# Gelu in phases on ScalarE, and Strassen's scheme for all but the first two token groups

## The chip, the cores and the metric

The kernel runs on one core of one Trainium2 chip. The metric is the time of the device in microseconds (us), median of the runs. A core has five engines that run beside each other and wait for one another through semaphores: TensorE (PE, matmuls; its weight loads are listed as PEld), VectorE (DVE), ScalarE (ACT), GpSimd (POOL) and SyncE (SP, which here issues stores). Each engine works through its own instructions in program order.

## The reference

Attention with causal mask over 8 batches, 8 heads, 576 tokens of 64 values, with 16 extra keys and values ("beacons") in front that every token sees; then a layer of two matrices with a gelu between, for all 4608 tokens.

```python
# q, k, v: (8, 8, 576, 64); beacon_k, beacon_v: (8, 8, 16, 64)
k_all = np.concatenate([beacon_k, k], axis=2)
v_all = np.concatenate([beacon_v, v], axis=2)
scores = scale * np.matmul(q, k_all.transpose(0, 1, 3, 2))      # scale = 1/8
scores = np.where(causal, -1e9, scores)
a = np.exp(scores - scores.max(-1, keepdims=True))
a /= a.sum(-1, keepdims=True) + 1e-09
attn = np.matmul(a, v_all)
x = attn.transpose(0, 2, 1, 3).reshape(4608, 512)

h = x @ w_in                                                    # (4608, 2048)
g = h * (1.0 / (1.0 + np.exp(-1.702 * h)))
out = g @ w_out                                                 # (4608, 512), float32
```

## The kernel before

The kernel is one Python function that first lists operations with their dependences, a guessed duration and a priority, lets a small planner (`Plan.run`) put them in order, and then writes the instructions in that order. The order on each engine is therefore fixed when the kernel is built; on the chip only semaphores move things.

The attention goes by 16 sets (a batch and four of its heads). The scores of a set are cut into chunks of at most 512 columns for each of the four heads; there are 55 chunks. A chunk is a burst of small matmuls (`qk`, L388) into one score tile, and one or two exponentials (L399) from it:

```python
pss = ctx.enter_context(tc.tile_pool(name="pss", bufs=1, space=bass.MemoryType.PSUM))
psu = ctx.enter_context(tc.tile_pool(name="psu", bufs=1, space=bass.MemoryType.PSUM))
RING = 4                                   # psu tiles u0..u3, [128, 512] f32 each
...
sc = pss.tile([P, Q, 512], F32, tag="s", name="s")
...
nc.scalar.activation(out=Es[s][:, :, c0:c1], in_=ss[i][...], func=AFT.Exp, scale=0.125)
```

There is one score tile, so the matmuls of a chunk wait for the exponential of the chunk before. All other matmul results go to a ring of four tiles `u`. GpSimd (and VectorE early on) masks the exponentials (L420), VectorE adds them up for the denominators (`zadd`, L451), and the value matmuls (`av`, L473) follow with transposes for the reciprocals (L484 to L493) and a multiplication (`norm`, L502) into `xT`, the input of the first layer.

The two layers go by ten groups of tokens: two of 256 (0 and 1), then eight of 512 (2 to 9). First layer (`m1`, L526): 16 tiles of 128 x 512 for a group of 512 tokens, four matmuls each. Then either tanh on ScalarE and a gate on VectorE, or gelu on ScalarE alone:

```python
def e_tanh(g, n0, n1):                                          # L540
    nc.scalar.activation(out=sig[:, 0:w], in_=rings[("m1", g, n0)][:, 0:w], func=AFT.Tanh, scale=0.851)
def e_gate(g, n0, n1):                                          # L559: (tanh + 1) * u
    nc.vector.scalar_tensor_tensor(out=gts[g][...], in0=sig, scalar=1.0, in1=u, op0=ALU.add, op1=ALU.mult)
def e_gelu(g, n0, n1):                                          # L547
    nc.scalar.activation(out=gts[g][...], in_=u, func=AFT.Gelu_apprx_sigmoid)
```

Groups from `GEL` on take gelu. Tanh and Exp share a table of ScalarE; gelu is in another, and the kernel before switches once, after the last exponential.

Second layer: a plain group takes 64 matmuls of 512 columns (`m2`, L571) and an evacuation on ScalarE (L584) for each 128 tokens. Groups from `NPL` up to `NPE` take Strassen's scheme: the 512 x 2048 by 2048 x 512 product is cut in quarters and made of seven products of 256-column matmuls (L640) in place of eight, with sums of quarters of `g` (`e_s`, L591, 16 pieces a group on VectorE) and of `w_out` (`e_t`, once), and joins of the results on VectorE (L656, seven a group) beside one halving on ScalarE (L651):

```python
NPL, NPE, GEL = 6, 10, 7
...
lhs, rhs = {
    1: (quarter(g, 0, 0), w(0, 0)), 2: (quarter(g, 0, 1), w(1, 0)), 3: (sA[2], w(1, 1)),
    4: (quarter(g, 1, 1), tb(2)),   5: (sA[0], tb(0)),   6: (sA[1], tb(1)),   7: (quarter(g, 1, 0), tb(3)),
}[p]
for n in range(n0, n1):
    for mt in range(2):
        nc.tensor.matmul(u[:, HM * mt : HM * (mt + 1)], lhs[:, n, mt * P : (mt + 1) * P], rhs[:, n, :], ...)
```

The chunks are spread by due times, so that the attention lasts until about two thirds of the span, with the layers of earlier tokens between them:

```python
T_ATT0, T_ATT1 = 13000, 235000            # ns; due time of chunk i rises evenly between them
```

Of the kernel before, what the change touches and what calls it, by code (L numbers as in the profile page):

```python
# [10 lines left out]
ALU = mybir.AluOpType  # L11


NEAR = 140


class Op:
    __slots__ = (
        "eng", "dur", "deps", "pr", "due", "emit", "kind", "ring", "mode", "lat",
        "start", "end", "left", "users", "ready", "seq", "name", "tail",  # L20
    )


class Plan:
# [5 lines left out]
    def __init__(self, ring):  # L30
        self.ops = []
        self.bank = [None] * ring
        self.tiles = {}
        self.closers = {}

    def op(self, eng, dur, deps, emit, kind="", pr=5, due=0, ring=None, closes=None, mode=None, name="", tail=0):
        o = Op()
        o.eng, o.dur, o.emit, o.kind, o.pr, o.due = eng, dur, emit, kind, pr, due
        o.ring, o.mode, o.name, o.tail = ring, mode, name, tail
# [23 lines left out]
    def run(self):  # L63
        free = {e: 0 for e in ("PE", "ACT", "DVE", "POOL", "Q", "SP")}
        free.update(POOL=900, SP=700)
        avail = {e: [] for e in free}
        for o in self.ops:
            if o.left == 0:
                avail[o.eng].append(o)
        mode, last, tail = "m", "", 0  # L70
        order = []
        todo = len(self.ops)
        while todo:
            best = None
            slot = self.ring_free()
            ringt = slot[0] if slot else None
            for e, cand in avail.items():
                t = None
                for o in cand:
                    r = max(o.ready, o.due)  # L80
# [12 lines left out]
            ok = []  # L93
            for o in avail[e]:
                r = max(o.ready, o.due)
                if o.ring is not None and o.ring not in self.tiles:
                    if ringt is None:
                        continue
                    r = max(r, ringt)
                if r <= t:  # L100
                    ok.append(o)
            if e == "PE":
                o = self.choose(ok, t, mode, last, free)
            else:
                o = min(ok, key=lambda o: (o.pr, o.ready, o.seq))
                if e == "DVE" and o.pr > 0:
                    near = [x for x in avail[e] if x.pr == 0 and max(x.ready, x.due) <= t + NEAR]
                    if near:
                        o = min(near, key=lambda o: (o.ready, o.seq))
                        t = max(t, o.ready, o.due)  # L110
            dur = o.dur
            if e == "PE":
                if o.mode != mode:
                    dur += 95 + 0.75 * tail / 2.4
                mode, last, tail = o.mode, o.kind, o.tail
                if o.ring is not None and o.ring not in self.tiles:
                    self.tiles[o.ring] = slot[1]
                    self.bank[slot[1]] = o.ring
            o.start, o.end = t, t + dur
# [17 lines left out]
    def choose(self, ok, t, mode, last, free):  # L137
        def first(kinds, test=lambda o: True):
            c = [o for o in ok if o.kind in kinds and test(o)]
            return min(c, key=lambda o: (o.pr, o.seq)) if c else None  # L140
# [9 lines left out]
                return av  # L150
        if qk:
            return qk
        late = first(("av",), lambda o: o.ready + 8000 <= t)
        if late:
            return late
        m1, m2 = first(("m1",)), first(("m2",))
        if m1 and m2:
            return m2 if last == "m1" or free["ACT"] > t + 1500 else m1
        return m1 or m2 or av
# [3 lines left out]
def kernel(  # L163
# [47 lines left out]
    w1t = cst.tile([P, NKT, DFF], F16, tag="w1", name="w1")  # L211
    w2t = cst.tile([P, NNT, DMODEL], F16, tag="w2", name="w2")
    XR = 4 * S
    NPL, NPE, GEL = 6, 10, 7
    HM, HN = 256, NNT // 2
    xT = cst.tile([P, NKT, XR], F16, tag="xT", name="xT")
    sA = [cst.tile([P, HN, HM], F16, tag=f"sA{i}", name=f"sA{i}") for i in range(3)]
# [375 lines left out]
    def tb(i):  # L593
        if i < 3:
            return tB[i][:, :, :]
        return bkf[:, :, :].bitcast(F16).rearrange("p s e -> p (s e)").rearrange("p (n w) -> p n w", w=HM)

    def e_t(i, eng):
        b11, b12 = w2t[:, 0:HN, 0:HM], w2t[:, 0:HN, HM:]
# [65 lines left out]
            in_=osbs[(g, i)][:, :].rearrange("p (a n) -> p a n", a=2),  # L665
        )

    T_ATT0, T_ATT1 = 13000, 235000
    NCH0 = 4 * HS
    T_CH = (T_ATT1 - T_ATT0) / (len(CHUNKS) - NCH0)  # L670

# [54 lines left out]
    def turns(s):  # L726
        urgent = s < HS
        cast = op(
            "DVE", 80, ld_bk[s] + [turn.get((s - 2, 1))], lambda: e_bk(s),
            pr=0 if urgent else 4, due=max(8800 * s if s < HS else 26000, due_of(s) - 10000), name=f"bk{s}",  # L730
        )
        bkc[s] = cast
        for which in (1, 0):
# [7 lines left out]
    def chunk(i):  # L741
# [6 lines left out]
        if i:  # L748
# [2 lines left out]
        w = sum(max(45, 2 * x / 2.4 + 6) for x in ps)  # L751
        qks[i] = op(
            "PE", w, deps, lambda: e_qk(i), kind="qk", pr=0,
            due=T_ATT0 + T_CH * (i - NCH0) if i >= NCH0 else 0, mode="r", name=f"qk{i}", tail=ps[-1],
        )
        for n, (s, c0, c1) in enumerate(CHUNKS[i]):
            x = exps[(i, n)] = op(
                "ACT", 140 + 0.833 * 4 * (c1 - c0), [qks[i]], lambda n=n: e_exp(i, n), pr=0, name=f"exp{s}.{i}"
            )
            parts.setdefault(s, []).append((c0, c1, x))  # L760
            for m, (j, a, e) in enumerate(MASKS):
# [9 lines left out]

    def after(s, c0, c1):
        return [x for u, v, x in parts[s] + masks.get(s, []) if u < c1 and v > c0]

    def values(s):
        b, hs = divmod(s, HS)
# [23 lines left out]
        for n, (x, half) in enumerate(order):  # L800
# [15 lines left out]
            )  # L816
            if x == 2:
                z1 = op("DVE", 410, [avs[(s, x, half)]], lambda h=half: e_z1(s, h), pr=0, closes=key, name="z1")
                z2[half] = op("DVE", 600, [z1], lambda h=half: e_z2(s, h), pr=0, name="z2")
            else:  # L820
                norms[(s, x, half)] = op(
                    "DVE", 380, [avs[(s, x, half)], z2[half]], lambda x=x, half=half: e_norm(s, x, half),
                    pr=1 if s >= HS else 0, closes=key, name="norm",
                )
# [34 lines left out]
    for j in range(-1, NJ):  # L859
        load_v(1, j)  # L860

    m1s, done, tanhs, gelus = {}, {}, [], []
    SQ, SDVE, TDUE = 2, 0, 200000

    def weights():
        prev = []
        for i in range(4):
            prev = [op("DVE", 1450, w2_ld + prev, lambda i=i: e_t(i, "DVE"), pr=3, due=TDUE, name="t")]
            tds[i] = prev[0]

    tds = {}

    def products(g):
        eng = "POOL" if g < SDVE else "DVE"
# [41 lines left out]
            op("SP", 60, [o], lambda: e_store4(g, i, r, c), name="store")  # L916

        prod(1)
        half = op("ACT", 560, [last[1]], lambda: e_half(g, 1, "m"), pr=1, closes=("p", g, 1), name="half")
        prod(2)  # L920
        c11 = join(2, "m", "a", [half])
        store(c11, "a", 0, 0)
# [11 lines left out]
        prod(3)  # L934
        c12 = join(3, "m", "m", [u4])
        store(c12, "m", 0, 1)

    def mlp(g):
        if g == NPL and NPL < NPE:
# [4 lines left out]
        for hb in range(t0 // HF, (t1 - 1) // HF + 1):  # L944
            b, half = divmod(hb, 2)
            for hs in range(HS):
                for x in range(2):
                    xs.append(norms[(HS * b + hs, x, half)])
        old = done.get(g - 2, [])
        n = 512 // w  # L950
        late = list(tanhs[-16:]) if g >= GEL else []
        firsts = list(range(0, NNT, n))
        if NPL <= g < NPE:
            firsts.sort(key=lambda n: (n % HN // SQ, n))
        for n0 in firsts:
# [6 lines left out]
            m1s.setdefault(g, []).append(pe)  # L962
            if g >= GEL:
                gates[(g, n0)] = op(
                    "ACT", 555 if gelus else 1840, [pe] + late, lambda n0=n0, n1=n1: e_gelu(g, n0, n1),
                    pr=1, closes=key, name="gelu",
                )
                gelus.append(gates[(g, n0)])
                continue
            a = op("ACT", 555, [pe], lambda n0=n0, n1=n1: e_tanh(g, n0, n1), pr=1, name="tanh")  # L970
            tanhs.append(a)
# [41 lines left out]
        o.left += 1  # L1013
        d.users.append(o)

    for o in bkc.values() if tds else ():
        also(tds[3], o)
    for o in gelus[:1]:
        for d in exps.values():
            also(o, d)  # L1020
    for o in gelus[1:]:
        also(o, gelus[0])
    order = plan.run()
    for o in order:
        o.emit()
# [29 lines left out]
```

## Time and profile before

| | before |
|---|---|
| time, median of 3 runs | 341.72 us (341.63 to 343.0) |
| span of the profiled run | 339.7 us, TensorE clock 0.999 |
| plain second layer (L571) | 320 matmuls of 512 columns |
| Strassen's products (L640) | 448 matmuls of 256 columns |
| gates on VectorE (L559) | 96, mean 678 ns |
| sums of quarters of `g` (L591) | 64, median 419 to 422 ns |
| joins (L656) | 28, mean 690 ns |
| tanh (L540), gelu (L547) | 96 of 598 ns, 48 of 597 ns |
| evacuations (L584) | 20, mean 598 ns |
| exponentials (L399) | 66, 98.8 us in all |

The page gives for each engine the time in which it was busy and its share of the span; then the span in 40 equal slices, one digit each, the busy share in tenths; then the chain of work that ended last, followed back from the last instruction, with the shares of engines. A row of the order in time gives start, length, engine, line, operation, output and inputs with their shapes, a count, and in brackets the idle time before it and what ended it. A row of the windows gives the stretch, its length, then busy time and count for PE, PEld, DVE, ACT and POOL, the granted clock, the share of DMA and GB/s. The modelled length of a matmul is longer than its distance to the next; distances between starts are the better measure.

### The profile page before, as it was taken

The page shows a single profiled execution, that of the slowest core. Times are in us where ns is not written, and L with a number is a line of the kernel's source. Part 1 is how long each engine was busy: PE and PEld are TensorE (multiplying, and loading weights), DVE is VectorE, ACT ScalarE, POOL GpSimd, SP SyncE. Part 2 cuts the span into 40 slices and gives each one's busy share as a digit, 9 for nine tenths or more (in the row PEclk, how much of TensorE's full clock was granted, in tenths as well). Part 3 has the DMA queues.
Part 4 walks back from the last instruction along what each step waited for, and adds up shares of the span by engine and source line. Part 5 has one row for each costly group of instructions (what it writes and reads, how often), then busy time and mean ns, then how long its engine had stood idle before and what let it go on. Part 6 is the DMA issues. An engine that isn't in the chain of part 4 may idle for free.

```text
span 339.7 us, 10091 instructions
## 1 busy us (share of the span) xinstructions
PE 318.0 (94%) x4360; PEld 196.9 (58%) x4360; DVE 246.8 (73%) x502; ACT 196.7 (58%) x236; POOL 117.5 (35%) x190
## 2 busy tenths in 40 slices
PE   0699898999889999999999999999999999999995
PEld 0475676544455455455566765455556766766784
DVE  3847869699989698897988999987762361371293
ACT  1585686778755776677767767767553244244200
POOL 8765585393245217442912563131100000000000
PEclk9999999999999999999999999999999999999999
DMA  7999999493419155905965191000000010010022
GB/s 129 159 206 208 194 204 139 97 92 83 67 41 138 36 102 59 147 33 102 84 94 101 40 150 51 31 35 33 33 0 33 32 64 31 33 63 33 32 95 93
DMA packets 56173, 28.84 MB, mean 85 GB/s; under 512 B 41280, under 2 KB 49472, under 8 KB 56128
## 3 DMA queue, kind: packets, MB, share of 16 engines
q0 software_dynamic: 47552, 18.49, 46.4%
q1 hardware_dynamic: 8512, 9.69, 8.2%
q8 instruction: 34, 0.56, 0.7%
q14 instruction: 11, 0.09, 0.1%
q10 hardware_dynamic: 64, 0.01, 0.0%
HBM read 37.22 MB, written 9.44 MB: 137 GB/s over the span
## 4 chain that ended last, share of the span: by engine, by line
PE 79%; DMA 9%; DVE 7%; POOL 2%; issue 1%; ACT 0%; DVEq 0%; POOLq 0%
PE u L526 32%; PE u L571 19%; PE u L640 14%; PE u L473 8%; PE s L388 7%; DMA w<-in_moe_w_in_dram 5%; DMA w<-in_moe_w_out_dram 4%; DVE g L559 2%; DVE zs L451 2%; DVE osb L656 1%; DVE xT L502 1%; DVE rz L493 1%; POOL vb L319 1%; POOL E L420 0%; ACT E L399 0%
## 5 line engine op out<-in xcount | busy, mean ns | idle before, releaser
L526 PE MATMUL u<-xT,w 128*128 128x512 f16 (+1 forms) x704 | 147.7, 341 | 1.2 <-DVE zt L484 0.5
L399 ACT ACTIVATE E<-s 128x2048 f16<-128x2048 f32 (+4 forms) x66 | 98.8, 1514 | 29.3 <-PE s L388 28.4
L526 PEld LDWEIGHTS <-w 128*128 128x128 f16 x704 | 66.3, 98 | 48.6 <-issue 1.3
L420 POOL TENSOR_SCALAR_AFFINE_SELECT E<-E 128x512 f16<-128x512 f16 (+3 forms) x90 | 53.1, 623 | 108.2 <-ACT E L399 97.9
L540 ACT ACTIVATE sig<-u 128x512 f16<-128x512 f32 x96 | 57.2, 598 | 45.2 <-PE u L526 42.4
L571 PE MATMUL u<-w,g 128*128 128x512 f16 x320 | 81.5, 380 | 0.4 <-DMA w<-in_moe_w_out_dram 0.3
L559 DVE SCALAR_TENSOR_TENSOR g<-sig,u 128x512 f16<-128x512 f16 x96 | 64.3, 678 | 20.6 <-ACT sig L540 20.2
L656 DVE SCALAR_TENSOR_TENSOR osb<-u,osb 128x512 f32<-128x512 f32 x28 | 18.9, 690 | 48.1 <-PE u L640 37.1
L547 ACT ACTIVATE g<-u 128x512 f16<-128x512 f32 x48 | 28.7, 597 | 43.1 <-PE u L526 43.0
L571 PEld LDWEIGHTS <-g 128*128 128x128 f16 x320 | 29.7, 98 | 31.9 <-issue 0.9
L388 PE MATMUL s<-qT,kT 32*128 32x32 f16 (+9 forms) x1544 | 35.9, 225 | 13.0 <-DVE qT L359 11.2
L388 PEld LDWEIGHTS <-kT 32*128 32x128 f16 x1544 | 28.5, 94 | 33.0 <-issue 20.7
L473 PE MATMUL u<-E,vb 128*32 128x288 f16 (+4 forms) x1024 | 29.4, 258 | 1.7 <-DVE g L559 1.2
L640 PEld LDWEIGHTS <-g 128*128 128x128 f16 x256 | 25.0, 98 | 10.4
L451 DVE TENSOR_TENSOR zs<-zs,E 128x192 f16<-128x192 f16 (+3 forms) x48 | 27.2, 568 | 4.2 <-POOL E L420 1.9
L319 POOL DMA_DIRECT2D vb<-in_v_dram x32 | 27.2, 865 | 2.4 <-DMA qn<-in_q_dram 1.2
L502 DVE TENSOR_TENSOR xT<-u,rz 128x288 f16<-128x288 f32 x64 | 26.4, 448 | 2.0 <-PE u L473 1.5
L473 PEld LDWEIGHTS <-vb 128*32 128x32 f16 (+1 forms) x1024 | 22.1, 98 | 5.9 <-issue 3.0
L640 PEld LDWEIGHTS <-sA 128*128 128x128 f16 x192 | 18.8, 98 | 4.7
L359 DVE STREAM_TRANSPOSE kT<-kn 128x576 f32<-128x576 f32 x16 | 20.1, 1258 | 1.9 <-DMA kn<-in_k_dram 1.4
L359 DVE STREAM_TRANSPOSE qT<-qn 128x576 f32<-128x576 f32 x16 | 20.0, 1248 | 0.4 <-DMA qn<-in_q_dram 0.3
L451 DVE TENSOR_TENSOR zs<-E 128x704 f16<-128x704 f16 (+1 forms) x24 | 16.0, 667 | 3.2 <-ACT E L399 2.6
(45 smaller groups left out, 210.0 us busy)
## 6 DMA issues: line engine op xcount, KB each, us to landing
out_dram<-osb SPq DMA_DIRECT2D x36, 256.0 KB, 2.2
kn<-in_k_dram POOLq DMA_DIRECT2D x16, 288.0 KB, 6.6
qn<-in_q_dram POOLq DMA_DIRECT2D x16, 288.0 KB, 6.3
vb<-in_v_dram POOLq DMA_DIRECT2D x24, 128.0 KB, 4.9
w<-in_moe_w_in_dram POOLq DMA_DIRECT2D x8, 256.0 KB, 9.7
w<-in_moe_w_out_dram POOLq DMA_DIRECT2D x4, 512.0 KB, 13.9
vb<-in_v_dram POOLq DMA_DIRECT2D x8, 112.0 KB, 3.7
vb<-in_v_dram POOLq DMA_DIRECT2D x8, 80.0 KB, 4.7
```

The costliest lines, as they stand in the source:

```text
L319: nc.gpsimd.dma_start(out=t[0 : hi - lo, j, h0:h1, :], in_=v[b, h0:h1, lo:hi, :].rearrange("h n d -> n h d"),)
L359: nc.vector.transpose(out=f32(dst.rearrange("p n e -> p (n e)")).rearrange("p (r t) -> p t r", t=TR), in_=f32(src[:, :]).rearrange("p (t c ...
L388: nc.tensor.matmul(sc[:, h, o : o + w], kT[s % NB2][r : r + 32, j * P : (j + 1) * P, d], qT[s % NB2][r : r + 32, a : a + w, d], start=(d = ...
L399: nc.scalar.activation(out=Es[s][:, :, c0:c1], in_=ss[i][:, :, o : o + c1 - c0], func=AFT.Exp, scale=0.125,)
L420: nc.gpsimd.affine_select(out=blk, in_=blk, compare_op=ALU.is_ge, fill=0.0, base=off + (Nb if j == 0 else 0), pattern=[[0, Q], [1, w]], ch ...
L451: nc.vector.tensor_tensor(out=t[:, :, o : o + w], in0=x, in1=y, op=ALU.add)
L473: nc.tensor.matmul(u[32 * h : 32 * h + 32, a:e], lhs, src[0:kw, h, col : col + e - a], start=first, stop=last,)
L526: nc.tensor.matmul(u[:, o + a - t0 : o + e - t0], w1t[:, kp, nt * P : (nt + 1) * P], xT[:, kp, a % XR : (e - 1) % XR + 1], start=(kp == 0) ...
L540: nc.scalar.activation(out=sig[:, 0:w], in_=rings[("m1", g, n0)][:, 0:w], func=AFT.Tanh, scale=0.851)
L559: nc.vector.scalar_tensor_tensor(out=gts[g][:, n0:n1, 0:w], in0=sigs[(g, n0)][:, 0 : n * w].rearrange("p (n w) -> p n w", n=n), scalar=1.0 ...
L571: nc.tensor.matmul(o[:, :], gts[g][:, nt, mt * P : (mt + 1) * P], w2t[:, nt, :], start=(nt == 0), stop=(nt == NNT - 1),)
L640: nc.tensor.matmul(u[:, HM * mt : HM * (mt + 1)], lhs[:, n, mt * P : (mt + 1) * P], rhs[:, n, :], start=(n == 0 and mt == 0), stop=(n == H ...
```

## The change

Strassen's scheme is used for groups 2 to 9 in place of 6 to 9, and gelu on ScalarE for the same groups in place of 7 to 9. It is meant to take matmuls from TensorE and gates from VectorE. As exponentials are still to come while those groups run, ScalarE must switch tables back and forth; so the planner gets phases. In an exponential phase there are chunks, values and second-layer products, but no first layer of the next group; when a given number of chunks is done (`QUOTAS`) and the group's input is ready, a gelu phase follows, with the 16 first-layer tiles of the group and no chunk.

```diff
-NEAR = 140
+NEAR = 260
...
+        def allowed(o):
+            if o.kind == "m2" and o.ring not in self.tiles:
+                if sum(left_of[k] > 0 for k in self.tiles if k in left_of) >= 2:
+                    return False
+            if o.kind == "m1":
+                return o.pr < group or (o.pr == group and (inside or group not in self.quota))
+            if o.kind == "qk":
+                return not inside
+            if o.table is not None and o.table != table:
+                return due_of_table[table] == 0
+            return True
...
+            if not inside and group in self.quota:
+                f = firsts[group]
+                inside = nchunk >= self.quota[group] and f.left == 0
...
+            if o.kind == "m1":
+                ntile += 1 if o.pr == group else 0
+                if inside and ntile == 16:
+                    group, inside, ntile = group + 1, False, 0
...
+                if o.table != table:
+                    dur += 1283
+                    table = o.table
...
-        late = first(("av",), lambda o: o.ready + 8000 <= t)
+        late = first(("av",), lambda o: o.ready + 6000 <= t)
...
+        if m1 and inside:
+            return m1
...
-    NPL, NPE, GEL = 6, 10, 7
+    NPL, NPE, GEL = 2, 10, 2
+    QUOTAS = (20, 26, 32, 41, 48, 55, 55, 55)
...
-        return bkf[:, :, :].bitcast(F16).rearrange("p s e -> p (s e)").rearrange("p (n w) -> p n w", w=HM)
+        return w2t[:, 0:HN, HM:]
...
-    T_ATT0, T_ATT1 = 13000, 235000
+    T_ATT0, T_ATT1 = 13000, 245000
...
-            due=T_ATT0 + T_CH * (i - NCH0) if i >= NCH0 else 0, mode="r", name=f"qk{i}", tail=ps[-1],
+            due=0, mode="r", name=f"qk{i}", tail=ps[-1],
...
-    SQ, SDVE, TDUE = 2, 0, 200000
+    SQ, SDVE, TDUE = 2, 0, 65000
...
-                    "ACT", 555 if gelus else 1840, [pe] + late, lambda n0=n0, n1=n1: e_gelu(g, n0, n1),
-                    pr=1, closes=key, name="gelu",
+                    "ACT", 555, [pe], lambda n0=n0, n1=n1: e_gelu(g, n0, n1),
+                    pr=1, closes=key, name="gelu", table="g",
...
-    for o in gelus[:1]:
-        for d in exps.values():
-            also(o, d)
+    plan.quota.update(zip(range(GEL, NG), QUOTAS))
```

A chunk has no due time of its own any more; the loads and transposes of its set still have. The sums of quarters of `w_out` move from 200 to 65 us in the plan, and the fourth of them now overwrites a quarter of `w_out` that only plain groups need. The rest of the diff passes the new fields along and adds two dependences that the planner had not listed.

More of the change, by code (lines that the diff above doesn't have):

```diff
@@ L19 @@
         "eng", "dur", "deps", "pr", "due", "emit", "kind", "ring", "mode", "lat",
-        "start", "end", "left", "users", "ready", "seq", "name", "tail",
+        "start", "end", "left", "users", "ready", "seq", "name", "tail", "table",
     )
@@ L34, in __init__, with op @@
         self.closers = {}
-    def op(self, eng, dur, deps, emit, kind="", pr=5, due=0, ring=None, closes=None, mode=None, name="", tail=0):
+        self.quota = {}
+    def op(self, eng, dur, deps, emit, kind="", pr=5, due=0, ring=None, closes=None, mode=None, name="", tail=0, table=None):
         o = Op()
         o.eng, o.dur, o.emit, o.kind, o.pr, o.due = eng, dur, emit, kind, pr, due
-        o.ring, o.mode, o.name, o.tail = ring, mode, name, tail
+        o.ring, o.mode, o.name, o.tail, o.table = ring, mode, name, tail, table
         o.deps = [d for d in deps if d is not None]
@@ L70, in run @@
         mode, last, tail = "m", "", 0
+        table, due_of_table = "e", {"e": 0, "g": 0}
+        group, inside, ntile, nchunk = min(self.quota), False, 0, 0
+        firsts = {}
+        for o in self.ops:
+            if o.kind == "m1":
+                firsts.setdefault(o.pr, o)
+        left_of = {}
+        for o in self.ops:
+            if o.kind == "m2":
+                left_of[o.ring] = left_of.get(o.ring, 0) + 1
+        def allowed(o):
[9 more added lines that the diff above has]
+            return True
         order = []
@@ L79, in run @@
                 for o in cand:
+                    if not allowed(o):
+                        continue
                     r = max(o.ready, o.due)
@@ L94, in run @@
             for o in avail[e]:
+                if not allowed(o):
+                    continue
                 r = max(o.ready, o.due)
@@ L102, in run @@
             if e == "PE":
-                o = self.choose(ok, t, mode, last, free)
+                o = self.choose(ok, t, mode, last, free, inside)
             else:
@@ L118, in run @@
                     self.bank[slot[1]] = o.ring
+            if o.kind == "m1":
+                ntile += 1 if o.pr == group else 0
+                if inside and ntile == 16:
+                    group, inside, ntile = group + 1, False, 0
+            if o.kind == "m2":
+                left_of[o.ring] -= 1
+            nchunk += o.kind == "qk"
+            if o.kind in ("m1", "qk"):
+                for u in o.users:
+                    if u.table is not None:
+                        due_of_table[u.table] += 1
+            if o.table is not None:
+                due_of_table[o.table] -= 1
+                if o.table != table:
+                    dur += 1283
+                    table = o.table
             o.start, o.end = t, t + dur
@@ L135, in run, with choose @@
         return order
-    def choose(self, ok, t, mode, last, free):
+    def choose(self, ok, t, mode, last, free, inside):
         def first(kinds, test=lambda o: True):
@@ L729, in turns @@
             "DVE", 80, ld_bk[s] + [turn.get((s - 2, 1))], lambda: e_bk(s),
-            pr=0 if urgent else 4, due=max(8800 * s if s < HS else 26000, due_of(s) - 10000), name=f"bk{s}",
+            pr=0 if urgent else 4, due=max(8800 * s if s < HS else 26000, due_of(s) - 8000), name=f"bk{s}",
         )
@@ L757, in chunk @@
             x = exps[(i, n)] = op(
-                "ACT", 140 + 0.833 * 4 * (c1 - c0), [qks[i]], lambda n=n: e_exp(i, n), pr=0, name=f"exp{s}.{i}"
+                "ACT", 140 + 0.833 * 4 * (c1 - c0), [qks[i]], lambda n=n: e_exp(i, n), pr=0, name=f"exp{s}.{i}",
+                table="e",
             )
@@ L773, in after, with two_back @@
         return [x for u, v, x in parts[s] + masks.get(s, []) if u < c1 and v > c0]
+    zseq = [(s, h) for h in range(2) for s in range(HS)]
+    zseq += [(s, h ^ (s >= ZSUM)) for s in range(HS, NSET) for h in range(2)]
+    def two_back(s, half):
+        i = zseq.index((s, half))
+        return zseq[i - 2] if i > 1 else (-1, 0)
     def values(s):
@@ L818, in values @@
                 z1 = op("DVE", 410, [avs[(s, x, half)]], lambda h=half: e_z1(s, h), pr=0, closes=key, name="z1")
-                z2[half] = op("DVE", 600, [z1], lambda h=half: e_z2(s, h), pr=0, name="z2")
+                z2[half] = op("DVE", 600, [z1] + [norms.get((*two_back(s, half), y)) for y in range(2)], lambda h=half: e_z2(s, h), pr=0, name="z2")
             else:
-                norms[(s, x, half)] = op(
+                norms[(s, half, x)] = op(
                     "DVE", 380, [avs[(s, x, half)], z2[half]], lambda x=x, half=half: e_norm(s, x, half),
@@ L860 @@
         load_v(1, j)
-    m1s, done, tanhs, gelus = {}, {}, [], []
-    SQ, SDVE, TDUE = 2, 0, 200000
+    m1s, done = {}, {}
+    SQ, SDVE, TDUE = 2, 0, 65000
     def weights():
@@ L867, in weights @@
         for i in range(4):
-            prev = [op("DVE", 1450, w2_ld + prev, lambda i=i: e_t(i, "DVE"), pr=3, due=TDUE, name="t")]
+            prev = [op("DVE", 1450, w2_ld + (prev if i < 3 else [tds[0]]), lambda i=i: e_t(i, "DVE"), pr=3, due=TDUE, name="t")]
             tds[i] = prev[0]
-    tds = {}
+    tds, ends = {}, {}
     def products(g):
@@ L918, in products @@
         prod(1)
-        half = op("ACT", 560, [last[1]], lambda: e_half(g, 1, "m"), pr=1, closes=("p", g, 1), name="half")
+        half = op("ACT", 560, [last[1], ends.get(g - 1)], lambda: e_half(g, 1, "m"), pr=1, closes=("p", g, 1), name="half")
         prod(2)
@@ L936, in products @@
         store(c12, "m", 0, 1)
+        ends[g] = c12
     def mlp(g):
@@ L947, in mlp @@
                 for x in range(2):
-                    xs.append(norms[(HS * b + hs, x, half)])
+                    xs.append(norms[(HS * b + hs, half, x)])
         old = done.get(g - 2, [])
         n = 512 // w
-        late = list(tanhs[-16:]) if g >= GEL else []
         firsts = list(range(0, NNT, n))
@@ L964, in mlp @@
                 gates[(g, n0)] = op(
-                    "ACT", 555 if gelus else 1840, [pe] + late, lambda n0=n0, n1=n1: e_gelu(g, n0, n1),
-                    pr=1, closes=key, name="gelu",
+                    "ACT", 555, [pe], lambda n0=n0, n1=n1: e_gelu(g, n0, n1),
+                    pr=1, closes=key, name="gelu", table="g",
                 )
-                gelus.append(gates[(g, n0)])
                 continue
-            a = op("ACT", 555, [pe], lambda n0=n0, n1=n1: e_tanh(g, n0, n1), pr=1, name="tanh")
-            tanhs.append(a)
+            a = op("ACT", 555, [pe], lambda n0=n0, n1=n1: e_tanh(g, n0, n1), pr=1, name="tanh", table="e")
             gates[(g, n0)] = op(
@@ L1014, in also @@
         d.users.append(o)
-    for o in bkc.values() if tds else ():
+    for o in done.get(NPL - 1, []) + done.get(NPL - 2, []) if tds else ():
         also(tds[3], o)
-    for o in gelus[:1]:
-        for d in exps.values():
-            also(o, d)
-    for o in gelus[1:]:
-        also(o, gelus[0])
+    plan.quota.update(zip(range(GEL, NG), QUOTAS))
     order = plan.run()
```

## The prediction

> **What bounds the kernel now.** I read the page from the top: engines and slices first, then the chain that ended last, then windows of the span, and last the order in time of TensorE and ScalarE where the two stages meet.
>
> ```profile
> PE 318.0 (94%) x4360; PEld 196.9 (58%) x4360; DVE 246.8 (73%) x502; ACT 196.7 (58%) x236; POOL 117.5 (35%) x190
> PE   0699898999889999999999999999999999999995
> DVE  3847869699989698897988999987762361371293
> ACT  1585686778755776677767767767553244244200
> ```
>
> TensorE is busy in nearly every slice. Its gaps are at the start (inputs and weights land until about 40 us) and in the last slice. VectorE runs at nine tenths from 60 to 240 us, so it is close behind.
>
> ```profile
> PE 79%; DMA 9%; DVE 7%; POOL 2%; issue 1%; ACT 0%; DVEq 0%; POOLq 0%
> ```
>
> The chain of waits runs through TensorE for 79% and through ScalarE for nothing. The windows say where TensorE has air:
>
> ```profile
> 40.00:130.00 90.00, 85.49 (x1404) 47.92 (x1406) 76.66 (x150) 64.83 (x72) 43.28 (x70) 1.00 0.79 102
> 130.00:240.00 110.00, 109.86 (x1682) 63.99 (x1683) 98.23 (x193) 76.69 (x88) 46.22 (x71) 1.00 0.50 72
> 240.00:317.00 77.00, 77.00 (x569) 49.13 (x568) 32.39 (x78) 32.34 (x54) 0.00 (x0) 1.00 0.10 35
> ```
>
> After the span's limits the first busy figure is TensorE, then weight loads, VectorE, ScalarE, GpSimd. TensorE idles 4.5 us between 40 and 130, 0.14 us between 130 and 240, nothing after. So the last 200 us shrink only if TensorE is given less to do. ScalarE, at 70% in the middle window, and VectorE, at 89%, can give way or get in the way, but saving on them alone moves nothing there.
>
> Lengths of the pieces, and the one place where the kernel already changes ScalarE's table between exponentials and gelu:
>
> ```profile
> 58.80 1.73 PE u L571 x8
> 317.92 15.30 PE u L640 x140
> 57.19 0.64 PE L388 MATMUL s<-qT,kT 32*128 32x288 f16 x24
> 57.96 1.88 ACT L399 ACTIVATE E<-s 128x2048 f16<-128x2048 f32 x1 [0.88 <-PE s L388]
> 244.00 1.28 ACT L547 ACT_TABLE_LOAD   x1
> 245.30 1.29 ACT L547 ACTIVATE g<-u 128x512 f16<-128x512 f32 x2
> ```
>
> Eight matmuls of 512 columns in 1.73 us are 216 ns each; 140 of Strassen's 256 columns in 15.30 us are 109.3 ns each. A chunk of scores takes 0.64 us of TensorE, its exponential begins 0.77 us after the chunk and lasts 1.88 us. The table load takes 1.28 us and the gelu follows at once.
>
> **What the Trainium skill says.** "ScalarE: Activation LUTs", What ACT_TABLE_LOAD costs: about 1283 ns for a load plus about 1380 ns of drain for every switch. The trace agrees with the first (1.28 us) and shows nothing of the second: the evacuation before it ends at 243.99, the load starts at 244.00, the gelu at 245.30. I charge 1.30 us. The same page, Table sets: the hidden batching unit, puts exp and tanh in one set and gelu in another; the trace agrees, as exponentials and tanh alternate without loads. "TensorE: Matmul & The Clock Gate", Back-to-back issue gap, gives N/2.4 + 2.5 ns, so 216 and 109 ns; the trace has 216 and 109.3. Halving the columns costs about 1 ns per matmul here, so nearly the whole of Strassen's saving arrives. "PSUM — Partial Sum Buffer", Specifications: eight banks of 512 FP32 values per partition. The score tile takes four (one buffer) and the ring of four tiles takes the rest, so no second score tile and no longer ring is to be had. That matters below.
>
> **The change part by part.**
>
> Second layer. A plain group is 64 matmuls of 512 columns: 64 x 216 = 13.84 us. With Strassen it is 7 products x 16 matmuls of 256 columns: 112 x 109.3 = 12.24 us. Saved on TensorE: 1.60 us a group. Four more groups (2 to 5): 6.4 us, all on the bound engine. First layer, scores and values keep their matmuls; the changes between the three tilings of the array, counted in the order of both kernels, are 145 before and 147 after, so nothing there.
>
> VectorE. Five groups (2 to 6) lose the gate: 80 x 0.67 us (64.3/96) = 53.6 us off. Four groups gain 16 additions of 0.42 us and 7 joins of 0.69 us: 4 x 11.5 = 46 us on. Net -7 us, about 239 us busy. No relief of note, and the additions stand beside the attention work where before they stood in the quiet last 90 us.
>
> ScalarE. Tanh for gelu is even (598 against 597 ns). Sixteen evacuations fall away and four halvings come: -7 us. The order shows six gelu phases, the last with three groups in it: 12 table loads instead of 2, +12.8 us. ScalarE rises to about 202 us of the span, far from a bound; what counts is where TensorE waits for a load.
>
> Rhythm of an exponential phase (seven chunks in each of the five full ones). One score tile, so the next chunk starts after the exponential: 0.77 + 1.88 + 0.05 = 2.70 us a chunk. The order puts about 20 Strassen matmuls (2.19 us) between two chunks, or values and some of them. TensorE: 0.58 for the chunk to its successor + 2.19 + about 0.1 for the change of tiling = 2.87. TensorE sets the pace by 0.2 us; the few thinner gaps (1.57, 1.82, 1.91) wait a few tenths. I put +0.5 us for all.
>
> Going into a gelu phase. From the start of the last chunk, 0.77 + 1.88 + 1.30 + 0.60 = 4.55 us until the first ring tile comes free. TensorE fills four tiles in 0.65 + 4 x 0.865 = 4.1 us, then waits about 0.5. In the order, two of the six entries have values or a rest of products to bridge this. 4 x 0.5 = +2 us.
>
> Coming out. The last gelu ends about 0.8 us after its matmuls, load 1.3, exponential 1.9: the second chunk can start 4.05 us after the last first-layer matmul. TensorE has one chunk (0.65) and 3.5 to 3.9 us of values and products there, 4.2 or more. Nothing lost.
>
> The stretch up to chunk 20. Groups 0 and 1 keep tanh and gate, group 2 is held back until 20 chunks are done, and the four sums of weights (about 1.5 us each on VectorE) move from 200 to 65 us. Twelve chunks of some 3 us VectorE work each stand here with about 11 gates, so VectorE is the tight engine: +1.5 us. Against it, the waits of TensorE for gates between 79 and 95 us in the kernel before (0.27, 0.58, 0.96, 0.19, about 2 us) go with the gates: -1.5.
>
> VectorE in the periods. One period (chunks and a gelu phase) is on TensorE 13.8 + 12.2 + 7 x 0.7 + values 4 = 35 us; VectorE has some 32 us in it, most of that in the exponential phase, since a join (0.69) must free a ring tile and a sum of exponentials must be ready for the values. I charge a few tenths per period, +1.5 us.
>
> Sum: -6.4 + 0.5 + 2 + 1.5 - 1.5 + 1.5 = -2.4, so 339.3. I think my charges lean to the high side, since the planner that fixes the order knows the load time, the ring and these durations and put bridging work where it could, and before it reached 109.86 of 110 us with VectorE at 89%. I halve the charges for the entries and VectorE's order (3.5 to 1.75) and take 337.4.
>
> **The rivals.**
>
> 1. Full gain: everything is bridged, and the waits before 130 us go too. Then -6.4 and up to -2 more: 333 to 335. For it: TensorE's order has work in each gap. Against: four entries with nothing between the first-layer matmuls and a ring of four.
>
> 2. VectorE becomes the bound in the middle. Its orders are fixed, and 32 us of work in 35 with joins, sums, transposes and additions in one queue lets one late item (a mask from GpSimd, an exponential) hold all behind it. In the trace the in-place sum of 1152 columns takes 996 ns against 779 for the one that writes elsewhere, so its length isn't steady. If it costs 1.5 us a period, 5 x 1.5 = 7.5 us: 342 to 345. For it: 17 to 19.7 us busy of each 20 already. Against: the mean load doesn't rise (53.6 off, 46 on).
>
> 3. ScalarE becomes the bound of the exponential phases. For it: the pace is only 0.2 us below TensorE's. If an exponential starts 0.4 us later than I think in each of 35 chunks, +7 us or more: 342 to 344. Against: 0.77 and 0.05 us are read in stretches where nothing else stood on ScalarE, and in these phases nothing but one halving does.
>
> 4. The loads of q, k and v come in bursts. For it: seven chunks in 20 us instead of one each 4.7. Against: DMA is at a twentieth to a tenth of its time after 80 us, and GpSimd idles half of it. No effect.
>
> **Range and chances.** 337.4, of which the certain part is the 6.4 us. The line for over 2% is 334.9, which leaves all losses together no more than the waits regained: rival 1, a bit over a quarter. Slower by over 2% (348.6) needs rivals 2 and 3 together at full size: one in twenty. Range 333 to 343.
>
> **What the profile would show.** Right: TensorE busy down by about 6 us; 320 plain matmuls of the second layer become 64, Strassen's 448 become 896; waits of the first-layer matmuls for gelu of about 0.5 us, once in each of some four phases; 12 table loads of 1.28 us. Rival 2: TensorE waiting for joins, sums or norms in the exponential phases, with VectorE full. Rival 3: chunks at more than 2.9 us from start to start with ScalarE full. The last 81 us, which I add up to from the order after the last chunk (48 first-layer tiles and 21 products), should be gapless. I am wrong if TensorE idles over 8 us in all after 40 us, or under 2.

## The result and the profile after

The changed kernel takes 333.49 us (333.26 to 333.51, four runs) against 342.36 us for the kernel before on the same chip (341.63 to 343.56, four runs): 0.9736 of the time, 95% interval 0.9702 to 0.977. (The median of three from which the prediction counts is 341.72; the fourth run took 343.56.) The spans of the two profiled runs are 339.7 and 331.8 us, 7.9 us apart.

The lines of the changed kernel's file are others than before: scores L439, exponentials L450, values L524, first layer L577, gelu L598, plain second layer L622, sums of quarters L642, Strassen's products L691 (L693 in e5 and e6), joins L707.

The page of the changed kernel, engines and slices, then the shares of the chain that ended last:

```profile
PE 312.2 (94%) x4552; PEld 215.6 (65%) x4552; DVE 239.8 (72%) x514; ACT 203.1 (61%) x234; POOL 117.3 (35%) x190
PE   0699998999999999999999999999999999999995
DVE  3747867898799779977899688977988600460483
ACT  1586586776866776778668576957676465065000
...
PE 70%; DMA 7%; issue 7%; POOL 7%; ACT 4%; DVE 3%; POOLq 0%; DVEq 0%
```

TensorE's busy time is down by 5.8 us, VectorE's by 7.0, ScalarE's is up by 6.4. Now the windows of the changed kernel (stretch, its length, busy time and count of PE, PEld, DVE, ACT, POOL, clock, DMA):

```profile
0.00:40.00 40.00, 27.69 (x547) 20.29 (x548) 26.55 (x58) 22.12 (x23) 28.11 (x49) 1.00 1.22 181
40.00:80.00 40.00, 37.85 (x602) 22.16 (x601) 31.83 (x58) 29.75 (x35) 23.03 (x36) 1.00 1.14 132
80.00:130.00 50.00, 49.62 (x813) 34.08 (x812) 42.85 (x93) 35.82 (x39) 18.64 (x31) 1.00 0.48 71
130.00:180.00 50.00, 49.72 (x825) 35.89 (x824) 43.77 (x97) 36.92 (x39) 25.16 (x40) 1.00 0.72 95
180.00:230.00 50.00, 50.00 (x742) 36.22 (x740) 40.17 (x90) 35.59 (x43) 14.15 (x23) 1.00 0.48 73
230.00:260.00 30.00, 29.43 (x498) 19.59 (x497) 26.08 (x59) 20.33 (x22) 8.18 (x13) 1.00 0.11 37
260.00:320.00 60.00, 60.00 (x466) 40.51 (x465) 22.28 (x52) 22.58 (x38) 0.00 (x0) 1.00 0.11 36
```

TensorE idles 0.38 us between 80 and 130, 0.28 us between 130 and 180, 0.57 us between 230 and 260 and nothing else up to 320. The kernel before idles 2.61 us between 80 and 130 (47.39 us busy of 50) and 1.90 between 40 and 80 (38.10 of 40). In the first 40 us the two kernels do the same work in nearly the same order; there the changed one idles 0.9 us less (27.69 us busy against 26.83), a difference of the size seen between other kernels of this document in that stretch.

How a gelu phase is entered, in TensorE's order in time and then in ScalarE's (start, length, engine, line, operation, output and inputs, count, and in brackets the idle time before and what ended it):

```profile
103.62 0.64 PE L439 MATMUL s<-qT,kT 32*128 32x176 f16 x32
104.20 3.63 PE L577 MATMUL u<-xT,w 128*128 128x512 f16 x16
108.17 4.04 PE L577 MATMUL u<-xT,w 128*128 128x512 f16 x18 [0.34 <-ACT g L598]
```
```profile
104.33 1.88 ACT L450 ACTIVATE E<-s 128x2048 f16<-128x2048 f32 x1 [1.69 <-PE s L439]
106.23 1.28 ACT L598 ACT_TABLE_LOAD   x1
107.52 3.17 ACT L598 ACTIVATE g<-u 128x512 f16<-128x512 f32 x6
```

The chunk starts at 103.62, its exponential at 104.33, the load at 106.23, the first gelu at 107.52. TensorE fills the four ring tiles with 16 matmuls and goes on at 108.17, which is 4.55 us after the chunk's start. The row shows 0.34 us of idle time, counted from the modelled end of the last matmul; by starts, 16 x 216 ns are over at 107.66, and 0.5 us are lost. Two more of the six entries wait, 0.41 us (at 71.78) and 0.36 us (at 249.50); the other three show no such wait.

### The profile page after: what moved, and what is told of

It reads as the page before. It is cut to its first block, busy times and chain, and to the rows that moved or that the text cites. A ratio compares the mean times of both kernels' runs of the same rounds, so it can differ in the third digit from the quotient of the medians.

```text
span 331.8 us, 10414 instructions
## 1 busy us (share of the span) xinstructions
PE 312.2 (94%) x4552; PEld 215.6 (65%) x4552; DVE 239.8 (72%) x514; ACT 203.1 (61%) x234; POOL 117.3 (35%) x190
## 4 chain that ended last, share of the span: by engine, by line
PE 70%; DMA 7%; issue 7%; POOL 7%; ACT 4%; DVE 3%; POOLq 0%; DVEq 0%
PE u L577 29%; PE u L691 25%; PE u L524 7%; PE s L439 6%; DMA w<-in_moe_w_out_dram 5%; ACT E L450 3%; PE u L622 3%; DMA w<-in_moe_w_in_dram 3%; POOL E L471 2%; POOL vb L370 2%; DVE osb L707 1%; DVE zs L502 1%; POOL qn L354 1%; POOL kn L354 1%; ACT L598 1%
## 5 line engine op out<-in xcount | busy, mean ns | idle before, releaser
L577 PE MATMUL u<-xT,w 128*128 128x512 f16 (+1 forms) x704 | 131.1, 343 | 1.4 <-ACT g L598 1.1
L450 ACT ACTIVATE E<-s 128x2048 f16<-128x2048 f32 (+4 forms) x66 | 98.8, 1514 | 50.7 <-PE s L439 50.0
L577 PEld LDWEIGHTS <-w 128*128 128x128 f16 x704 | 67.6, 98 | 56.9 <-issue 2.4
L598 ACT ACTIVATE g<-u 128x512 f16<-128x512 f32 x128 | 74.4, 599 | 46.0 <-PE u L577 31.7
L707 DVE SCALAR_TENSOR_TENSOR osb<-u,osb 128x512 f32<-128x512 f32 x56 | 37.7, 681 | 39.7 <-issue 26.5
L691 PEld LDWEIGHTS <-g 128*128 128x128 f16 x512 | 48.9, 98 | 7.0
L439 PE MATMUL s<-qT,kT 32*128 32x32 f16 (+9 forms) x1544 | 36.0, 227 | 12.4 <-DVE qT L410 10.9
L439 PEld LDWEIGHTS <-kT 32*128 32x128 f16 x1544 | 28.9, 95 | 27.2 <-issue 14.5
L691 PE MATMUL u<-w,g 128*128 128x256 f16 x384 | 46.0, 273 | 0.0
L691 PEld LDWEIGHTS <-sA 128*128 128x128 f16 x384 | 36.2, 98 | 5.2
L691 PE MATMUL u<-tB,sA 128*128 128x256 f16 x256 | 32.1, 273 | 0.0
L524 PE MATMUL u<-E,vb 128*32 128x288 f16 (+4 forms) x1024 | 28.5, 257 | 0.3 <-DVE xT L553 0.3
L524 PEld LDWEIGHTS <-vb 128*32 128x32 f16 (+1 forms) x1024 | 21.8, 97 | 4.7 <-issue 1.9
L642 DVE TENSOR_TENSOR sA<-g 128x512 f16<-128x512 f16 x32 | 13.1, 426 | 14.5 <-ACT g L598 14.5
L535 DVE STREAM_TRANSPOSE zt<-u 128x288 f32<-128x288 f32 x32 | 14.0, 464 | 7.6 <-PE u L524 7.2
```

Source lines behind the costliest of these rows:

```text
L439: nc.tensor.matmul(sc[:, h, o : o + w], kT[s % NB2][r : r + 32, j * P : (j + 1) * P, d], qT[s % NB2][r : r + 32, a : a + w, d], start=(d = ...
L450: nc.scalar.activation(out=Es[s][:, :, c0:c1], in_=ss[i][:, :, o : o + c1 - c0], func=AFT.Exp, scale=0.125,)
L524: nc.tensor.matmul(u[32 * h : 32 * h + 32, a:e], lhs, src[0:kw, h, col : col + e - a], start=first, stop=last,)
L577: nc.tensor.matmul(u[:, o + a - t0 : o + e - t0], w1t[:, kp, nt * P : (nt + 1) * P], xT[:, kp, a % XR : (e - 1) % XR + 1], start=(kp == 0) ...
L598: nc.scalar.activation(out=gts[g][:, n0:n1, 0:w], in_=rings[("m1", g, n0)][:, 0 : n * w].rearrange("p (n w) -> p n w", n=n), func=AFT.Gelu ...
L707: nc.vector.scalar_tensor_tensor(out=osbs[(g, dst)][:, :], in0=rings[("p", g, p)][:, :], scalar=scale_of(g), in1=osbs[(g, src)][:, :], op0 ...
```

## The experiments

Theory: TensorE sets the time, Strassen's columns are the gain, the table loads hide, and gelu is there to make room on VectorE. Rivals: the gain is a better order; VectorE or ScalarE is close to being the bound. The kernel before, run beside each set of experiments, took 342.36 (with the changed kernel), 341.49 (e1 to e4) and 341.35 us (e5 to e8), so a difference of about 1 us between sets is not resolved by the times alone; where a smaller one matters, the traces decide.

**Gelu in phases alone (e1).**

```diff
-    NPL, NPE, GEL = 2, 10, 2
+    NPL, NPE, GEL = 6, 10, 2
```

> The changed kernel with Strassen only for groups 6 to 9, as before; gelu and its phases for groups 2 to 9. Theory (Strassen's fewer columns bring 1.60 us a group, gelu in phases brings only the waits for gates): four groups lose 6.4 us of TensorE, so 333.5 + 6.4 = 340, some 2 us under the kernel before. Rival A (the gain is the phases: fewer interruptions and no gates, Strassen's saving is eaten by joins and sums): about 335. Rival B (phases cost, Strassen brings over 8 us): 342 to 344.

Measured: 340.35 us, 0.9955 of the kernel before (0.9939 to 0.9971). The phases with gelu alone bring half a per cent, and the other 6.9 us (340.35 - 333.49) come with the four further Strassen groups. Adding up in the traces, for each kind of matmul, the time from one matmul's start to the next less the idle time (gaps of 0.15 us and more), the second layer takes 122.5 us in this run and 116.2 us in the changed kernel: 6.3 us, for 6.4 expected. This is the theory's result. The whole of that sum, in us:

| | before | e1 | changed |
|---|---|---|---|
| start of the first matmul | 8.2 | 8.4 | 8.4 |
| scores | 32.4 | 31.7 | 32.4 |
| values | 36.9 | 34.7 | 35.1 |
| first layer | 129.1 | 128.3 | 128.7 |
| second layer, plain and Strassen | 120.1 | 122.5 | 116.2 |
| idle after the first matmul | 9.2 | 9.5 | 7.2 |
| after the last matmul | 3.9 | 3.9 | 3.9 |

A change of tiling is booked to the matmul ahead of it: one of 512 columns before a chunk takes 312 ns to the chunk's start in place of 216. A matmul of the second layer stands just before a chunk 15 times in the kernel before and 34 times in e1, so from before to e1 that row grows, by 2.4 us in all, while the values shrink by 2.2; before and e1 can be compared in their totals, not row by row. Of the 2.3 us of idle time between e1 and the changed kernel, 1.6 lie in the first 40 us, where the orders hardly differ.

**Strassen for groups 2 to 9 without gelu and phases (e2).** Tanh and gates for groups 2 to 6, gelu after the last exponential, due times of before.

```diff
-    NPL, NPE, GEL = 2, 10, 2
-    QUOTAS = (20, 26, 32, 41, 48, 55, 55, 55)
+    NPL, NPE, GEL = 2, 10, 7
+    QUOTAS = (55, 55, 55)
-    T_ATT0, T_ATT1 = 13000, 245000
+    T_ATT0, T_ATT1 = 13000, 235000
-            due=0, mode="r", name=f"qk{i}", tail=ps[-1],
+            due=T_ATT0 + T_CH * (i - NCH0) if i >= NCH0 else 0, mode="r", name=f"qk{i}", tail=ps[-1],
```

> Strassen for groups 2 to 9 with the due times of before and tanh with gates for groups 2 to 6, gelu only after the last exponential; no phases. VectorE then has the gates (about 54 us) and the sums and joins (46 us) together. Theory (gelu is needed to make room on VectorE): VectorE has about 293 us of work, nearly all of it before 260 us, so it becomes the bound: 350 to 365. Rival (VectorE has room, Strassen alone brings its 6.4 us): 334 to 337.

Measured: 357.81 us, 1.0477 of before (1.0427 to 1.0526). Its windows:

```profile
80.00:130.00 50.00, 43.42 (x712) 28.88 (x712) 48.39 (x103) 28.51 (x30) 17.71 (x30) 0.97 0.48 71
130.00:180.00 50.00, 46.20 (x721) 29.01 (x721) 49.02 (x104) 29.88 (x37) 19.06 (x33) 1.00 0.49 71
```

VectorE is busy 48.4 and 49.0 of 50 us, TensorE only 43.4 and 46.2. The list of waits (engine, line, what it waited for: us in total, times, longest) names the gates, L610 here:

```profile
PE u L577 <- DVE g L610: 6.2, 8, 1.8
PE u L524 <- DVE g L610: 2.3, 4, 0.8
```

After 40 us TensorE waits 13.3 us for VectorE in this run, 8.5 of them for gates, and 4.1 us for exponentials. The matmuls saved are given back as waits. Gelu in phases is worth little by itself (e1), and without it Strassen for these groups loses. This run takes away gelu and phases together; an order made for Strassen with gates was not tried.

**No phases (e3).** First-layer tiles and chunks may mix, and ScalarE switches whenever nothing of its present table is due.

```diff
-        group, inside, ntile, nchunk = min(self.quota), False, 0, 0
+        group, inside, ntile, nchunk = 99, False, 0, 0
-            due=0, mode="r", name=f"qk{i}", tail=ps[-1],
+            due=T_ATT0 + T_CH * (i - NCH0) if i >= NCH0 else 0, mode="r", name=f"qk{i}", tail=ps[-1],
```

> The changed kernel without phases: first-layer tiles and chunks may mix, and the planner switches tables when nothing of the present table is due: 36 loads in place of 12. Theory (each entry into gelu costs TensorE some tenths because the ring of four fills during exponential, load and first gelu): 24 more loads, 31 us more on ScalarE and 12 more entries with 0.4 to 3 us each: 340 to 360. Rival (loads are hidden whatever their number, since ScalarE has a third of its time free): 333 to 336.

Measured: 377.58 us, 1.104 of before (1.0998 to 1.1082), beyond the theory's span. ScalarE's order in time in this run:

```profile
94.19 1.28 ACT L450 ACT_TABLE_LOAD   x1
95.48 1.88 ACT L450 ACTIVATE E<-s 128x2048 f16<-128x2048 f32 x1
97.37 1.28 ACT L598 ACT_TABLE_LOAD   x1
98.67 1.08 ACT L598 ACTIVATE g<-u 128x512 f16<-128x512 f32 x2
99.77 1.28 ACT L450 ACT_TABLE_LOAD   x1
101.06 1.88 ACT L450 ACTIVATE E<-s 128x2048 f16<-128x2048 f32 x1
```

One exponential and two gelus make a round of 5.58 us (from the load at 94.19 to that at 99.77), 2.57 of them loads, and nothing is idle between. In the same stretch TensorE waits for ScalarE once or twice a round: 1.25, 1.12, 0.61, 1.25 us. So here ScalarE does become the bound, from 80 to 130 us, busy 48.16 of 50. But the run's 44 us over the changed kernel are not all loads. After 40 us TensorE waits 16.9 us for ScalarE and 15.6 us for VectorE, whose order is another too; the longest single wait is for a transpose of queries:

```profile
194.30 1.04 PE L439 MATMUL s<-qT,kT 32*128 32x256 f16 x32 [3.94 <-DVE qT L410]
```

And the clock fell (see the end). What the 36 loads alone cost was not separated. What is shown is that 12 in phases cost under 2 us (next run), and that an order without phases, with 36, loses far more.

**No loads (e4).** The order on TensorE and VectorE is the changed kernel's; tanh stands in for gelu, so that 11 of the 12 loads go. Gelu itself is left out.

```diff
-            func=AFT.Gelu_apprx_sigmoid,
+            func=AFT.Tanh,
```

> The changed kernel in the same order on TensorE and VectorE, with tanh in place of gelu in groups 2 to 9, so that only one table load of 12 is left; what it leaves out is gelu itself (its output is of tanh). Theory: the loads cost only the waits of about 0.4 us at three of six entries: 1.1 us, so 332.4. Rival (each of 11 loads costs its 1.28 us or half of it): 319 to 327.

Measured: 331.56 us, 0.97 of before (0.9664 to 0.9737), 1.9 us under the changed kernel. The three waits for the first gelu of a phase are gone, about 1.6 us by starts, and this is the firmer figure: the times are of two sets of runs. (A wait of 1.31 us at 55.97, before any switch to gelu, reads 0.90 here, and the first matmul starts 0.4 us later; neither is due to the loads.) The 14 us of loads (11 x 1.28) are hidden but for some 1.6.

**VectorE loaded further (e5 and e6).** Two of the four sums of quarters made twice (e5) and four times (e6), with the same result.

```diff
         elif i == 1:
-            add(eng, s2, s1, a11, ALU.subtract)
+            for _ in range(2):          # e6: range(4)
+                add(eng, s2, s1, a11, ALU.subtract)
         elif i == 2:
-            add(eng, s4, a12, s2, ALU.subtract)
+            for _ in range(2):          # e6: range(4)
+                add(eng, s4, a12, s2, ALU.subtract)
```

> The changed kernel with two of the four sums of quarters of g made twice, with the same result, and the order otherwise kept: 8 more instructions of about 0.4 us a group on VectorE, 3.2 us a group, 26 us in all. Theory (VectorE has room in each period, about 3 us or more, mostly in the gelu phases where the sums stand): 333.5 to 336. Rival (VectorE is at its limit in the periods with attention): five periods of 3.2 us, 345 to 350.

Measured: 337.14 us, 0.987 of before (0.9843 to 0.9898): 3.6 us more than the changed kernel (2.7 between the spans of the profiled runs) for 25 us more work (265.06 us busy against 239.80). Windows and TensorE's order in time of e5:

```profile
80.00:130.00 50.00, 49.54 (x813) 34.14 (x811) 47.57 (x106) 35.65 (x39) 18.84 (x31) 1.00 0.48 73
130.00:180.00 50.00, 49.70 (x824) 35.86 (x823) 47.19 (x105) 36.84 (x39) 24.88 (x40) 1.00 0.71 92
```
```profile
249.44 2.75 PE L577 MATMUL u<-xT,w 128*128 128x512 f16 x12 [0.36 <-ACT g L598]
...
321.52 0.61 PE L693 MATMUL u<-tB,sA 128*128 128x256 f16 x4 [0.18 <-DVE sA L642]
...
325.63 1.05 PE L693 MATMUL u<-w,g 128*128 128x256 f16 x8 [1.31 <-DVE g L642]
```

The entry that the changed kernel reaches at 249.50 us is reached here at 249.44. With VectorE at 47.57 and 47.19 us of 50, the five periods with attention lose nothing. Waits of TensorE for the sums show only in the last 20 us: the sums of group 9 must wait for the products of group 8, which read the same buffers, so there they stand on the path. The theory's room of 3 us a period holds, and my rival of the prediction, that one late item on a full VectorE holds all behind it, falls for this load. The sums stand mostly in the gelu phases; the same work added beside the chunks was not tried.

> The same with these sums made four times: 24 more instructions a group, about 9.6 us a group. By either theory VectorE is now over its limit: if its room is 3 to 5 us a period, five periods lose 5 to 7 us each, 355 to 370. If it stays under 345, VectorE has much more room than its busy time says.

Measured: 385.08 us, 1.1275 of before (1.1243 to 1.1308), more than either figure. Two of its windows, and lines of TensorE's order in time:

```profile
80.00:130.00 50.00, 43.81 (x670) 28.67 (x669) 47.13 (x109) 31.03 (x35) 14.64 (x24) 0.93 0.42 63
130.00:180.00 50.00, 41.66 (x548) 27.29 (x547) 47.00 (x108) 26.50 (x29) 14.88 (x23) 0.90 0.41 58
```
```profile
87.16 2.85 PE L524 MATMUL u<-E,vb 128*32 128x288 f16 x64 [3.17 <-DVE zt L535]
...
133.38 4.42 PE L693 MATMUL u<-w,g 128*128 128x256 f16 x20 [4.88 <-DVE xT L553]
```

TensorE now waits 3 to 5 us at a time for VectorE in the middle. 3 us of extra work a period cost nothing there and 10 us cost much; where between them the room ends was not measured. VectorE's busy share does not tell the two apart: it is 47.57 and 47.19 of 50 us in e5, where TensorE has 49.5 and 49.7, and 47.13 and 47.00 here, where TensorE has 43.8 and 41.7. The lower clock of this run (0.93 and 0.90 in these windows) is part of its loss.

**The planner's numbers in the kernel before (e7).**

```diff
-NEAR = 140
+NEAR = 260
-        late = first(("av",), lambda o: o.ready + 8000 <= t)
+        late = first(("av",), lambda o: o.ready + 6000 <= t)
-    T_ATT0, T_ATT1 = 13000, 235000
+    T_ATT0, T_ATT1 = 13000, 245000
```

> The kernel before with only the planner's three numbers of the change (NEAR 260, value matmuls late after 6000, attention until 245000); no gelu phase and no further Strassen group. Theory (they only fit the order to the phases): 340 to 344, the same. Rival (a good part of the gain is a better order): 336 to 339.

Measured: 342.41 us, 1.0019 of before (1.0002 to 1.0036): the same. These numbers bring nothing by themselves. What else the diff changes in the order (one due time, a limit on open tiles of the second layer, the added dependences) is not in this run, but all of it is in e1, which gains 0.5%.

**One number of the changed kernel (e8).**

```diff
-    SQ, SDVE, TDUE = 2, 0, 65000
+    SQ, SDVE, TDUE = 2, 0, 75000
```

> The changed kernel with one number changed: the sums of quarters of w_out are planned for 75 us in place of 65 us. They take 6 us of VectorE in all and their first user, product 6 of group 2, comes at about 90 us. Theory (TensorE is full and has other work): within 1 us, 333 to 335. Rival (the order as a whole is fragile, one number moves many instructions behind it): 337 to 341.

Measured: 337.92 us, 0.9903 of before (0.987 to 0.9936), 4.4 us more than the changed kernel. My theory was wrong here and the rival right. TensorE's order in time of e8:

```profile
94.70 0.66 PE L439 MATMUL s<-qT,kT 32*128 32x256 f16 x32
...
98.61 1.05 PE L691 MATMUL u<-w,sA 128*128 128x256 f16 x8
100.69 0.65 PE L439 MATMUL s<-qT,kT 32*128 32x288 f16 x24 [1.04 <-ACT E L450]
101.27 0.38 PE L524 MATMUL u<-zs,ones 128*32 128x288 f16 x8
101.48 0.23 PE L524 MATMUL u<-E,ones 128*32 128x80 f16 x8
103.35 0.66 PE L439 MATMUL s<-qT,kT 32*128 32x208 f16 x40 [1.64 <-ACT E L450]
103.94 1.62 PE L524 MATMUL u<-E,vb 128*32 128x288 f16 x64
106.09 0.65 PE L439 MATMUL s<-qT,kT 32*128 32x176 f16 x32 [0.53 <-ACT E L450]
```

Between 87.47 and 94.70 TensorE had run 60 product matmuls in a row without a chunk; so the products were used up by 99.6 us and the last three chunks of the phase had only values beside them. Then the bare rhythm shows: 100.69, 103.35, 106.09, one chunk each 2.7 us, with 1.04, 1.64 and 0.53 us of waits for the exponentials: 3.2 us of the 3.8 by which the spans of the profiled runs differ (335.6 and 331.8). The changed kernel spreads the same products over all seven chunks and waits for none of them in this phase. In VectorE's order of e8 the last two sums of weights now stand between 86.3 and 89.6 us and a transpose of keys behind them, at 92.97 to 94.22, just ahead of the late chunk. That the sums pushed this transpose, and it the chunk, is how I read it; it wasn't tried.

## Why the prediction was right, point by point

The time lies half a microsecond inside the lower end of the range, at the first rival (full gain, 333 to 335), and not at 337.4. The mechanism and its main term held. The terms for waits did not: they added to a loss, and the waits fell. Two charges, both for VectorE, were far too large, and one gain too small.

- Strassen, -6.4 us: the second layer falls by 6.3 us between e1 and the changed kernel, the time by 6.9. Right. The section of the Trainium skill that the prediction names for the spacing ("TensorE: Matmul & The Clock Gate", Back-to-back issue gap) gives that formula for single matmuls and about 131 ns for 512 columns in streams of weight loads and matmuls; here such streams take 216 ns (eight in 1.73 us), so in this kernel the formula holds and the lower figure does not.
- Entries into gelu phases, "4 x 0.5 = +2 us": the chain of 4.55 us to the first free tile is 4.55 at 103.62, and the loss of an entry is 0.5 us by starts. But three entries wait, not four: 1.6 us, and in e4 these waits are gone with the loads. Halving this charge was wrong. (The table in the Trainium skill, "ScalarE: Activation LUTs", Table sets: the hidden batching unit, has gelu and not the kernel's `Gelu_apprx_sigmoid`, which it calls separate; that this function too is in another set than Exp is shown by the loads themselves, 12 here and 36 in e3.)
- Rhythm of the exponential phases, +0.5 us: one wait for an exponential, 0.21 us at 244.91 (another, 0.43 at 63.90, lies ahead of the first gelu phase). Right that it is small. That TensorE sets the pace only as long as products lie between the chunks is shown by e8.
- "The stretch up to chunk 20 ... +1.5 us": TensorE idles 2.15 us between 40 and 80 against 1.90, and 0.41 of the 2.15 is the entry at 71.78. So there is next to nothing of this term. I took a busy VectorE for a late one.
- Waits for gates regained, -1.5 us: the trace of before has 2.3 us of TensorE waiting for gates after 40 us, that of the changed kernel none.
- "VectorE in the periods ... +1.5 us": one wait of 0.28 us for a norm. This is the term that failed by kind: I charged a few tenths a period because I put VectorE at 32 of 35 us (it is busy 43 to 44 of 50); e5 adds 3 us a period and TensorE still arrives at 249.44 us.
- The sum: with the halved charges the terms add to -4.15, so 337.55 and not quite 337.4; the spans differ by 7.9. TensorE's busy time falls by 5.8 us. Its idle time between 40 and 320 us falls from 4.64 to 3.38 us, by 1.3, where the terms for waits add to +2.25: these 3.5 us are nearly the whole miss. In the first 40 us it falls by 0.9, which is luck as far as these runs show: that idle time runs from 12.3 to 14.0 us over kernels with nearly the same order there. Without it the time would still lie in the range.
- The signs that the prediction names: 64 plain matmuls and 896 of Strassen's, 12 loads, busy time down by 5.8 us came as said. The last 81 us have the one wait of 0.36 us at 249.50. TensorE idles 7.3 us after 40 us, within the 2 to 8 set; but 3.9 of these come after the last matmul, and the kernel before has 8.5 by the same count, so this sign told little.
- The rival "ScalarE becomes the bound" was seen in the order of e3, and "VectorE becomes the bound" in that of e2 and in e6: both were real cliffs beside the path, neither was on it. Against the rival of the loads the prediction puts DMA at a twentieth to a tenth of its time after 80 us; its own window from 130 to 240 us shows 0.50. The conclusion stands all the same: after 40 us the trace of the changed kernel names no transfer in any wait of TensorE.

Between 40 and 320 us TensorE has 3.4 us of gaps left in the changed kernel, those at the three entries among them; the 12 us at the start and the 3.9 us after the last matmul are outside this change.

## What to carry to other kernels

If one engine is full, count what a change takes off it, and charge other engines only for waits that the full engine would see: here VectorE at 43 of 50 us cost nothing, at 47 of 50 nothing in the middle, and with 10 us more a period, again at 47 of 50, the kernel lost 52 us (what the lower clock adds included). So a busy share does not say how much room is left; adding work to the engine in steps, as e5 and e6 do, shows it. Table switches cost what their chain (last exponential, load, first gelu) sticks out over the buffers that the busy engine may still fill; grouped into phases it was some 1.6 us for 11 loads. And a change that pays on one engine may need another that pays nothing alone (gelu in phases 0.5% faster, Strassen alone 4.8% slower, both 2.6% faster): test them together before dropping one.

## What was not expected of the hardware

In some stretches where TensorE's work has gaps, the granted clock is lower too, and that adds to the loss. The windows of e3 (180 to 230 us) show TensorE busy only 38.56 of 50 us, at a clock of 0.86:

```profile
180.00:230.00 50.00, 38.56 (x665) 32.34 (x657) 37.54 (x80) 27.64 (x29) 16.17 (x26) 0.86 0.48 70
```

In TensorE's order in time of the same run, eight first-layer matmuls take 3.14 us from start to start (114.11 to 117.25), 392 ns each on average in place of 216. The windows around them put the clock at 0.50 for 3.41 us and at 1.00 before and after:

```profile
114.11 3.21 PE L577 MATMUL u<-xT,w 128*128 128x512 f16 x8 [0.61 <-DVE zt L535]
117.25 0.66 PE L439 MATMUL s<-qT,kT 32*128 32x224 f16 x32
```
```profile
105.00:113.41 8.41, 6.46 (x156) 4.76 (x154) 4.76 (x8) 8.06 (x9) 3.85 (x5) 1.00 0.03 4
113.41:116.82 3.41, 2.80 (x19) 1.09 (x8) 3.27 (x10) 3.38 (x3) 3.23 (x6) 0.50 1.21 77
116.82:125.00 8.18, 7.37 (x152) 5.01 (x150) 6.64 (x14) 7.98 (x8) 4.49 (x7) 1.00 1.18 147
```

TensorE had waited 1.51 us (until 111.40) and 0.22 us (until 113.19) shortly before that stretch.

The mean clock was 0.968 in e3, 0.956 in e6 and 0.995 in e2, against 1.0 in the changed kernel. So a lost microsecond on TensorE can cost more than itself. It is not so in every stretch with gaps (e2 between 130 and 180 us: 46.20 of 50 busy, clock 1.00; e3 between 90 and 110 us, with the waits of up to 1.25 us quoted above: clock 1.00), and what gap it takes was not measured.
